# Turning queries with VectorE's 32x32 transposes, and spreading k's maxima through DRAM

## The chip, the cores and the metric

The kernel runs on one core of one Trainium2 chip. The metric is the device time of one execution in microseconds. Three runs of the kernel before gave a median of 943.58 us (943.5 to 944.65).

The engines have these names in the profile: PE is TensorE (matrix products and transposes; PEld its weight loads), DVE is VectorE, ACT is ScalarE, POOL is GpSimd, and SP is the engine whose queue issues nearly all DMAs. SBUF is the on-chip memory with 128 partitions; PSUM holds what PE writes.

## The reference

There are 8 batches, 8 heads, 576 positions and a head width of 64. Queries go through a softmax over the width, keys through a softmax over the positions; there is no attention matrix, only a 64x64 product for each head. The result, 4608 tokens of 512 features, goes through two dense layers with 2048 features between them.

```python
q_s = np.exp(q - np.max(q, axis=-1, keepdims=True))
q_s = q_s / (np.sum(q_s, axis=-1, keepdims=True) + 1e-09)
k_s = np.exp(k - np.max(k, axis=2, keepdims=True))
k_s = k_s / (np.sum(k_s, axis=2, keepdims=True) + 1e-09)
kv = np.einsum('bhsd,bhse->bhde', k_s, v)
x = np.einsum('bhsd,bhde->bhse', q_s, kv)      # then (batch, position) x (head, width)
h = x @ w_in
out = (h * np.clip(h + 3.0, 0.0, 6.0) / 6.0) @ w_out
```

## The kernel before

**Blocks and units.** The 4608 tokens are cut into 9 blocks of 512 (`TB`). As a batch has 576 tokens, block j takes its first 64 j tokens from batch j-1 and the others from batch j. The heads are taken in four pairs, `hp`, of 128 features. One unit, `attention(j, hp)`, does the attention part of one block for one pair of heads. It is a generator, and its `yield`s cut it into steps:

1. It loads k, v and q of the unit, takes k's maxima (`km`) and does the softmax of the queries (`q_softmax`).
2. It subtracts k's maxima from k and takes the exponential, and it turns the queries from tokens x features to features x tokens and splits them into a high and a low part (`qT_hi`, `qT_lo`).
3. It computes `kv` (`kv_of`, ten matmuls into `pkv`, for which the matrix `ke` must be ready).
4. It multiplies `kv` with the turned queries (`px`) and splits the result into `x_hi` and `x_lo`, the input of the dense layers.

**Precision.** Products in the dense layers and, from block 2 on, in step 4 are made of three passes over high and low parts, which `split` makes: ACT writes the high part, DVE (or POOL for some of the weights) subtracts.

**The dense layers.** For each block, 16 groups `f` of 128 hidden features: `gemm1(j, f)` has 12 matmuls into `ph`, then ACT and DVE form the activation `g` (L351, L352) and its parts `g_hi` and `g_lo` (L111, L112). `gemm2`, one group behind, adds 12 matmuls into the four banks `po`. At the end of a block `store` copies the four banks into `ob` (two buffers, by ACT and DVE in turn) and SP sends them out.

**The order of the work.** The units of block j+1 run between the groups of block j, one step for each group: step 1 comes with f = 0, 4, 8 and 12, step 2 with the next f, and so on. Blocks 0 and 1 are "early": block 0's attention comes before everything, block 1's during block 0, while the weights are still being loaded and decoded (`decode`, which uses DVE, ACT and POOL). From block 1 of the dense layers on, PE's instructions stay in the order of the program (`keep_in_program_order`). On all other engines, and on SP's queue, a planner that simulates the times of the instructions sets the order, and it moves work ahead as far as the buffers allow: `kt` and `kb` have one buffer, `ke`, `vt`, `qt` and `km` two. Each engine and SP's queue then run strictly in the order that the planner chose.

**k's maxima, from block 2 on.** k is loaded twice: `kt` with features on the partitions, for the maxima (L286), and `ke` with positions on the partitions, for the product. The maxima come out as one number on each partition, and they are needed along the free dimension on all partitions. POOL copies them to a 128x128 square `kb` (L288), PE transposes it into PSUM as `pm` (L297, through `flip`, L85), and DVE subtracts from `ke` (L298). ACT takes the exponential (L301).

**The queries, from block 2 on.** A tile `qt` has 128 tokens on the partitions and 4 x 128 values in each. `q_softmax` works on groups of 64 values: a maximum (L238), a subtraction (L239), an exponential (L240), a sum (L241), a reciprocal with a small term added (L242, L243) and a multiplication (L244). In step 2 PE transposes the four 128x128 squares into `tp`, and `split` reads them from PSUM.

Of the kernel before, what the change touches and what calls it, by code (L numbers as in the profile page):

```python
# [10 lines left out]
F32 = mybir.dt.float32  # L11
F32R = mybir.dt.float32r
U32 = mybir.dt.uint32
AF = mybir.ActivationFunctionType
ALU = mybir.AluOpType
AX = mybir.AxisListType
PSUM = bass.MemoryType.PSUM

P = 128
TB = 512  # L20
NC4 = TB // P
EPS = 1e-9
LOWEST = float(np.finfo(np.float32).min)
# [6 lines left out]
def attention_moe(  # L30
    ctx: ExitStack,
    tc: tile.TileContext,
    q: bass.AP,
    kT: bass.AP,
    k: bass.AP,
    v: bass.AP,
# [12 lines left out]

    nc = tc.nc

    NB, NP = q.shape[:2]
    B, S = kT.shape[0], kT.shape[3]
    D = q.shape[5]
    NT, DM = out.shape
    NFC = w.shape[0]
    NCC = DM // P
    NTT = TB // P  # L60
    NCH = S // P + 1
    TAIL = S % P
    SHIFT = S - TB

    const = ctx.enter_context(tc.tile_pool(name="const", bufs=1))
    wp = ctx.enter_context(tc.tile_pool(name="wp", bufs=1))
    att = ctx.enter_context(tc.tile_pool(name="att", bufs=1))
    xp = ctx.enter_context(tc.tile_pool(name="xp", bufs=2))
    moe = ctx.enter_context(tc.tile_pool(name="moe", bufs=2))
    ps_a = ctx.enter_context(tc.tile_pool(name="ps_a", bufs=2, space=PSUM))  # L70
    ps_h = ctx.enter_context(tc.tile_pool(name="ps_h", bufs=2, space=PSUM))
    ps_o = ctx.enter_context(tc.tile_pool(name="ps_o", bufs=4, space=PSUM))
# [11 lines left out]
    def flip(out, in_):  # L84
        ordered(nc.tensor.transpose(out, in_, ident))  # L85
# [15 lines left out]

    late = iter(range(NFC - 1, -1, -1))

# [5 lines left out]
    def split(hi, lo, src, engine=nc.vector):  # L109

        nc.scalar.copy(hi, src)  # L111
        engine.tensor_sub(lo, src, hi.bitcast(F32))  # L112
# [44 lines left out]
    def x_block(j):  # L157
        if j not in x_tiles:
            x_tiles[j] = (
                xp.tile([P, NCC, TB], F32R, name=f"x_hi{j}", tag="x_hi"),  # L160
                xp.tile([P, NCC, TB], F32R, name=f"x_lo{j}", tag="x_lo"),
            )
# [13 lines left out]
    def load_first(hp):  # L176
        t = borrow(f"kq{hp}")
        kt, qt, qT = t[:, 0:S], cut(t, S, NC4, 2, D), t[:, S + TB : S + 2 * TB]
        nc.sync.dma_start(kt, kT[0, hp])
# [8 lines left out]
    def kv_of(j, hp, ke, vt):  # L188
# [3 lines left out]
        for c in range(NCH):  # L192
            r = slice(0, P if c < NC4 else TAIL)
            mm(pv, ke[r, c, :], vt[r, c, :, :], c == 0, c == NCH - 1)
# [21 lines left out]

    n8 = 2 * NC4

# [3 lines left out]
    def q_softmax(qt, lean, pool):  # L222

        qs = qt.rearrange("p c h d -> p (c h) d")
        qm = att.tile([P, n8], F32, name="qm", bufs=2)
        qr = att.tile([P, n8], F32, name="qr", bufs=2)
        if lean:
            nc.vector.tensor_reduce(qm, qs, axis=AX.X, op=ALU.max, negate=True)
            for i in range(n8):
                nc.scalar.activation(  # L230
                    qs[:, i],
                    qs[:, i],
                    AF.Exp,
                    bias=qm[:, i : i + 1],
                    accum_out=qr[:, i : i + 1],
                )
        else:
            nc.vector.tensor_reduce(qm, qs, axis=AX.X, op=ALU.max)  # L238
            pool.tensor_sub(qs, qs, over(qm))  # L239
            nc.scalar.activation(qs, qs, AF.Exp)  # L240
            nc.vector.tensor_reduce(qr, qs, axis=AX.X, op=ALU.add)  # L241
        nc.vector.tensor_scalar_add(qr, qr, EPS)  # L242
        nc.vector.reciprocal(qr, qr)  # L243
        pool.tensor_mul(qs, qs, over(qr))  # L244

    def k_softmax(j, km, ke, kt):
# [6 lines left out]
        pe2 = pool.tile([P, TB], F32, name="pe2", tag=tag)  # L253
        for c in range(NC4):
            flip(pe[:, c * P : (c + 1) * P], kt[:, c * P : (c + 1) * P])
        flip(pe2[0:TAIL, 0:P], kt[:, TB:S])
        nc.scalar.copy(ke[:, 0:NC4].rearrange("p c n -> p (c n)"), pe)
        nc.scalar.copy(ke[0:TAIL, NC4], pe2[0:TAIL, 0:P])

    def attention(j, hp):  # L260

        early = j < 2
        if not j:
            kt, qt, qT, vt, ke = first[hp]
        else:
            if j < B:
                kt = att.tile([P, S], F32, name="kt", bufs=1)  # L270
                nc.sync.dma_start(kt, kT[j, hp])
                ke = att.tile([P, NCH, P], F32, name="ke", bufs=2)
                if not early:
                    nc.sync.dma_start(ke, k[j, hp].rearrange("p c h d -> p c (h d)"))
                vt = att.tile([P, NCH, 2, D + 1], F32, name="vt", bufs=2)
                nc.sync.dma_start(vt, v[j, hp])
            qt = att.tile([P, NC4, 2, D], F32, name="qt", bufs=2)
            nc.sync.dma_start(qt, q[j, hp])

        if j < B:  # L280
            km = att.tile([P, 1], F32, name="km", bufs=2)
            if early:
                ks = k_softmax(j, km, ke, kt)
                next(ks)
            else:
                nc.vector.tensor_reduce(km, kt, axis=AX.X, op=ALU.max)  # L286
                kb = att.tile([P, P], F32, name="kb", bufs=1)
                nc.gpsimd.tensor_copy(kb, km.broadcast_to([P, P]))  # L288
        q_softmax(qt, j == 1, nc.vector if j else nc.gpsimd)
        yield  # L290

        if early:
            next(ks, None)
        elif j < B:

            pm = ps_a.tile([P, TB], F32, name="pm", tag="pa")
            flip(pm[:, 0:P], kb)  # L297
            nc.vector.tensor_sub(  # L298
                ke, ke, pm[:, 0:P].rearrange("p (o n) -> p o n", o=1).broadcast_to([P, NCH, P])
            )  # L300
            nc.scalar.activation(ke, ke, AF.Exp)  # L301
        pool, tag = (ps_a, "pa") if j else (ps_o, "po")
        tp = pool.tile([P, TB], F32, name="tp", tag=tag)
        for c in range(NC4):
            flip(tp[:, c * P : (c + 1) * P], qt[:, c].rearrange("p h d -> p (h d)"))
        if early:
            if j:
                qT = att.tile([P, TB], F32, name="qT", tag="qT_hi")
            nc.scalar.copy(qT, tp)
        else:  # L310
            qT_hi = att.tile([P, TB], F32R, name="qT_hi")
            qT_lo = att.tile([P, TB], F32R, name="qT_lo")
            split(qT_hi, qT_lo, tp)
        yield

        if j < B:
            kv_of(j, hp, ke, vt)
            if not early:
                kv_split(j, hp)
            yield  # L320


        pool, tag = (ps_a, "pa") if j else (ps_h, "ph")
        px = pool.tile([P, TB], F32, name="px", tag=tag)
        e = SHIFT * j
        for b, lo, hi in ((j - 1, 0, e), (j, e, TB)):
            if lo < hi:
                c = slice(lo, hi)
                if early:
                    mm(px[:, c], kvs[b, hp], qT[:, c], True, True)  # L330
                else:
                    kv_hi, kv_lo = kvs[b, hp]
                    mm(px[:, c], kv_hi, qT_hi[:, c], True, False)
                    mm(px[:, c], kv_hi, qT_lo[:, c], False, False)
                    mm(px[:, c], kv_lo, qT_hi[:, c], False, True)
        x_hi, x_lo = x_block(j)
        split(x_hi[:, hp, :], x_lo[:, hp, :], px)
        if j == 1:
            kv_split(j, hp)
# [18 lines left out]
    def gemm2(f, g_hi, g_lo, po):  # L358
        first, last = f == 0, f == NFC - 1
        passes = [  # L360
# [50 lines left out]
    for j in range(NB):  # L411
        for f in range(NFC):
            if j == 0:
# [4 lines left out]
            g = gemm1(j, f)  # L418
# [24 lines left out]
def _laid_out(q, k, v, moe_w_in, moe_w_out):  # L443

    B, H, S, D = q.shape
    NP, NCH = H // 2, S // P + 1
    tokens = q.transpose(0, 2, 1, 3).reshape(B * S // TB, NC4, P, NP, 2, D)
    pad = ((0, 0), (0, 0), (0, NCH * P - S), (0, 0))

    def by_chunk(a):  # L450
        return a.reshape(B, NP, 2, NCH, P, a.shape[-1]).transpose(0, 1, 4, 3, 2, 5)

    ones = np.ones((B, H, S, 1), v.dtype)
    n, m = moe_w_in.shape
    w_in = moe_w_in.reshape(n // P, P, m // P, P).transpose(2, 1, 0, 3).reshape(m // P, P, n)
    w = np.stack([w_in, moe_w_out.reshape(m // P, P, n)], axis=2)
    if w.dtype != np.float64:
        raise TypeError(w.dtype)
    return {
        "q": tokens.transpose(0, 3, 2, 1, 4, 5),  # L460
        "kT": k.transpose(0, 1, 3, 2).reshape(B, NP, 2 * D, S),
        "k": by_chunk(np.pad(k, pad, constant_values=LOWEST)),
        "v": by_chunk(np.pad(np.concatenate([v, ones], axis=-1), pad)),
        "w": np.ascontiguousarray(w).view(np.uint64),
    }
# [27 lines left out]
```

## Time and profile before

| what | value |
|---|---|
| median of the runs | 943.58 us |
| the profiled execution's own time | 944.06 us |
| its span, first to last instruction | 942.2 us |
| granted clock, mean | 0.996 |
| PE busy | 915.0 us, 97% |
| DVE busy | 475.9 us, 51% |
| ACT busy | 347.3 us, 37% |
| POOL busy | 34.2 us, 4% |
| chain that ended last | PE 85%, DVE 5% |

The durations in the profile come from the one profiled execution. "Busy" is the share of the span in which an engine had at least one instruction running; matmuls overlap, so the sum of their durations is larger than their share of the time. In a row of the timeline, the brackets hold how long the engine was idle before the instruction and what released it.

### The profile page before, as it was taken

The numbers are of one execution on the slowest core, as the hardware profiler recorded it, in microseconds if no ns is written. First come the engines' busy times: TensorE is split into PE (matmuls) and PEld (weight loads), VectorE is DVE, ScalarE is ACT, GpSimd is POOL, SyncE is SP. The second block draws the span as 40 slices with busy tenths as digits, with TensorE's granted clock in tenths as the row PEclk, the third lists the DMA queues.
The fourth block names the chain that finished last, engine by engine and source line by source line (L and its number), as shares of the span: only waits on it lengthen the run. The fifth ranks groups of instructions, "written<-read, shape, count | busy, mean of one in ns | idle before, by whom it ended". The sixth has DMA issues, their size and how long they took to land.

```text
span 942.2 us, 10586 instructions
## 1 busy us (share of the span) xinstructions
PE 915.0 (97%) x4164; PEld 740.1 (79%) x4164; DVE 475.9 (51%) x823; ACT 347.3 (37%) x599; POOL 34.2 (4%) x49
## 2 busy tenths in 40 slices
PE   5799989999999999999999999999999999999998
PEld 4577767888888888888888888888888888888886
DVE  6999995444444445444544444444444444222222
ACT  6998543223323333333333332323332332222222
POOL 3022110000000000000000000000000000000000
PEclk9999999999999999999999999999999999999999
DMA  9941312111211112111211121112110010001001
GB/s 365 415 187 44 102 35 69 52 52 42 86 51 52 52 52 98 52 52 52 97 53 43 34 97 52 41 41 83 53 40 12 12 56 12 1 1 45 0 1 45
DMA packets 25537, 64.29 MB, mean 68 GB/s; under 512 B 2832, under 2 KB 2832, under 8 KB 23568
## 3 DMA queue, kind: packets, MB, share of 16 engines
q1 hardware_dynamic: 24912, 62.57, 19.1%
q10 hardware_dynamic: 576, 1.05, 0.3%
q8 instruction: 33, 0.54, 0.2%
q14 instruction: 16, 0.13, 0.0%
HBM read 54.17 MB, written 9.44 MB: 68 GB/s over the span
## 4 chain that ended last, share of the span: by engine, by line
PE 85%; DVE 5%; ACT 0%; issue 0%; DVEq 0%; ACTq 0%
PE po L82 39%; PE ph L82 39%; PE pkv L82 3%; PE px L82 2%; PE tp L85 1%; DVE v L141 1%; DVE v L145 1%; DVE m L136 1%; DVE qt L244 0%; DVE m L134 0%; DVE g_lo L112 0%; DVE g L352 0%; PE pm L85 0%; DVE w L112 0%; DVE x_lo L112 0%
## 5 line engine op out<-in xcount | busy, mean ns | idle before, releaser
L82 PE MATMUL ph<-x_hi,w 128*128 128x512 f32 x1152 | 389.1, 399 | 5.4 <-ACT w L111 2.3
L82 PE MATMUL po<-w,g_hi 128*128 128x512 f32 x1152 | 302.1, 400 | 3.8 <-ACT g_hi L111 3.8
L82 PEld LDWEIGHTS ph<-x_hi,w 128*128 128x128 f32 x1152 | 216.9, 189 | 60.4 <-ACT w L111 4.2
L352 DVE SCALAR_TENSOR_TENSOR g<-g,ph 128x512 f32<-128x512 f32 x144 | 98.6, 685 | 322.1 <-ACT g L351 322.1
L82 PEld LDWEIGHTS po<-w,g_hi 128*128 128x128 f32 x1152 | 210.6, 188 | 52.4 <-ACT g_hi L111 5.7
L351 ACT ACTIVATE g<-ph,three 128x512 f32<-128x512 f32 x144 | 98.9, 687 | 395.6 <-PE ph L82 395.6
L82 PE MATMUL ph<-x_lo,w 128*128 128x512 f32 x576 | 228.2, 396 | 0.0
L82 PE MATMUL po<-w,g_lo 128*128 128x512 f32 x576 | 161.6, 394 | 0.0
L82 PEld LDWEIGHTS ph<-x_lo,w 128*128 128x128 f32 x576 | 109.2, 190 | 26.0 <-issue 0.6
L82 PEld LDWEIGHTS po<-w,g_lo 128*128 128x128 f32 x576 | 107.9, 188 | 26.2 <-DVE g_lo L112 0.5
L112 DVE TENSOR_TENSOR g_lo<-g,g_hi 128x512 fp32r<-128x512 f32 x144 | 101.1, 702 | 32.2 <-ACT g_hi L111 29.7
L111 ACT CAST g_hi<-g 128x512 fp32r<-128x512 f32 x144 | 89.3, 620 | 61.0 <-DVE g L352 59.5
L298 DVE TENSOR_TENSOR ke<-ke,pm 128x640 f32<-128x640 f32 x24 | 19.7, 821 | 54.4 <-PE pm L85 54.4
L82 PEld LDWEIGHTS pkv<-vt,ke 128*128 128x128 f32 x280 | 37.4, 189 | 5.8
L82 PE MATMUL pkv<-vt,ke 128*128 128x130 f32 x280 | 41.2, 284 | 0.0
L240 ACT ACTIVATE qt<-qt 128x512 f32<-128x512 f32 x28 | 17.7, 633 | 63.7 <-DVE qt L239 63.7
L241 DVE TENSOR_REDUCE qr<-qt 128x8 f32<-128x512 f32 x28 | 19.2, 685 | 18.2 <-ACT qt L240 18.2
L288 POOL COPY kb<-km 128x128 f32<-128x128 f32 x24 | 7.0, 293 | 564.4 <-PE pm L85 560.8
L112 DVE TENSOR_TENSOR x_lo<-px,x_hi 128x512 fp32r<-128x512 f32 x36 | 24.6, 686 | 0.1
L244 DVE TENSOR_TENSOR qt<-qt,qr 128x512 f32<-128x512 f32 x32 | 24.3, 760 | 0.5
L133 ACT ACTIVATE m<-raw 128x1024 f32<-128x1024 f32 x16 | 18.4, 1147 | 12.3 <-DVE v L141 12.1
L112 POOL TENSOR_TENSOR w<-v,w 128x1024 fp32r<-128x1024 f32 x7 | 17.8, 2541 | 105.3 <-ACT w L111 105.3
(74 smaller groups left out, 547.4 us busy)
## 6 DMA issues: line engine op xcount, KB each, us to landing
raw<-in_w_dram SPq DMA_DIRECT2D x15, 1024.0 KB, 14.7
out_dram<-ob SPq DMA_DIRECT2D x36, 256.0 KB, 2.0
vt<-in_v_dram SPq DMA_DIRECT2D x28, 325.0 KB, 3.5
qt<-in_q_dram SPq DMA_DIRECT2D x32, 256.0 KB, 2.6
kt<-in_kT_dram SPq DMA_DIRECT2D x28, 288.0 KB, 2.8
ke<-in_k_dram SPq DMA_DIRECT2D x24, 320.0 KB, 2.9
kv<-in_v_dram SPq DMA_DIRECT2D x4, 325.0 KB, 6.5
kq<-in_kT_dram SPq DMA_DIRECT2D x4, 288.0 KB, 5.2
```

The costliest lines, as they stand in the source:

```text
L82: ordered(nc.tensor.matmul(out, lhsT, rhs, start=start, stop=stop))
L85: ordered(nc.tensor.transpose(out, in_, ident))
L111: nc.scalar.copy(hi, src)
L112: engine.tensor_sub(lo, src, hi.bitcast(F32))
L133: nc.scalar.activation(m, high.bitcast(F32), AF.Abs)
L136: nc.vector.tensor_scalar(m, m, 3, 0x3FFFFFFF, op0=ALU.logical_shift_left, op1=ALU.bitwise_and)
L240: nc.scalar.activation(qs, qs, AF.Exp)
L241: nc.vector.tensor_reduce(qr, qs, axis=AX.X, op=ALU.add)
L244: pool.tensor_mul(qs, qs, over(qr))
L298: nc.vector.tensor_sub(ke, ke, pm[:, 0:P].rearrange("p (o n) -> p o n", o=1).broadcast_to([P, NCH, P]))
L351: nc.scalar.activation(g, ph, AF.Relu, bias=three, scale=1.0)
L352: nc.vector.scalar_tensor_tensor(g, g, 6.0, ph, op0=ALU.min, op1=ALU.mult)
```

## The change

The change has two parts, both for the units of block 2 and later. Blocks 0 and 1 keep the old way.

**Queries.** They come in another layout, `qf`, prepared outside of the chip as `q` was. Partition 32 r + t holds, for each of 16 groups `g` of 32 tokens, the 32 values of quarter r of the pair's 128 features for token t of that group. Half a head stands on one partition and its other half on the partition 32 away. So the maxima and the sums are taken over 32 values (16 of each per partition), and `both_halves` joins the halves: POOL copies four pieces of 32 partitions to the neighbouring quarter, and DVE combines the result with its own. It is called twice for each unit, for the maxima and for the sums. When the softmax is done, DVE's `transpose` turns each 32x32 square, and the tile has features on the partitions and tokens along the free dimension. Its target `qT` uses buffers of the tag "v", which `decode` uses too. `split` then reads `qT` in SBUF instead of `tp` in PSUM. PE's four transposes and `tp` go.

**k's maxima.** SP writes `km` to a small tile in DRAM (`kd`) and reads it back into `kb` on all 128 partitions. DVE subtracts from `ke` with `kb` as its operand. POOL's copy, PE's transpose and `pm` go.

```diff
+    dr = ctx.enter_context(tc.tile_pool(name="dr", bufs=2, space=bass.MemoryType.DRAM))
...
+    NG = TB // QD
+
+    def across(t):
+        return t.rearrange("p (g o) -> p g o", o=1).broadcast_to([P, NG, QD])
+
+    def both_halves(stat, op):
+        swap = att.tile([P, NG], F32, name="swap", bufs=2)
+        for r in range(0, P, QD):
+            o = r ^ QD
+            nc.gpsimd.tensor_copy(swap[r : r + QD], stat[o : o + QD])
+        nc.vector.tensor_tensor(stat, stat, swap, op=op)
+
+    def q_softmax_t(qt):
+        qs = qt.rearrange("p (g d) -> p g d", d=QD)
+        qm = att.tile([P, NG], F32, name="qm", bufs=2)
+        qr = att.tile([P, NG], F32, name="qr", bufs=2)
+        nc.vector.tensor_reduce(qm, qs, axis=AX.X, op=ALU.max)
+        both_halves(qm, ALU.max)
+        nc.vector.tensor_sub(qs, qs, across(qm))
+        nc.scalar.activation(qt, qt, AF.Exp)
+        nc.vector.tensor_reduce(qr, qs, axis=AX.X, op=ALU.add)
+        both_halves(qr, ALU.add)
+        nc.vector.tensor_scalar_add(qr, qr, EPS)
+        nc.vector.reciprocal(qr, qr)
+        nc.vector.tensor_mul(qs, qs, across(qr))
+        qT = moe.tile([P, 2 * DM], F32, name="v", bufs=2)[:, 0:TB]
+        nc.vector.transpose(qT, qt)
+        return qT
...
-            qt = att.tile([P, NC4, 2, D], F32, name="qt", bufs=2)
-            nc.sync.dma_start(qt, q[j, hp])
+            qt = att.tile([P, TB], F32, name="qt", bufs=2)
+            nc.sync.dma_start(qt, q[j, hp] if early else qf[j - 2, hp])
...
                 nc.vector.tensor_reduce(km, kt, axis=AX.X, op=ALU.max)
+
+                kd = dr.tile([P], F32, name="kd")
+                nc.sync.dma_start(kd.rearrange("(p o) -> p o", o=1), km)
                 kb = att.tile([P, P], F32, name="kb", bufs=1)
-                nc.gpsimd.tensor_copy(kb, km.broadcast_to([P, P]))
-        q_softmax(qt, j == 1, nc.vector if j else nc.gpsimd)
+                nc.sync.dma_start(
+                    kb, kd.rearrange("(o n) -> o n", o=1).broadcast_to([P, P])
+                )
+        if early:
+            q_softmax(qt, j == 1, nc.vector if j else nc.gpsimd)
+        else:
+            qT = q_softmax_t(qt)
         yield
...
-            pm = ps_a.tile([P, TB], F32, name="pm", tag="pa")
-            flip(pm[:, 0:P], kb)
             nc.vector.tensor_sub(
-                ke, ke, pm[:, 0:P].rearrange("p (o n) -> p o n", o=1).broadcast_to([P, NCH, P])
+                ke, ke, kb.rearrange("p (o n) -> p o n", o=1).broadcast_to([P, NCH, P])
             )
...
-            split(qT_hi, qT_lo, tp)
+            split(qT_hi, qT_lo, qT)
```

More of the change, by code (lines that the diff above doesn't have):

```diff
@@ L20 @@
 TB = 512
+QD = 32
 NC4 = TB // P
@@ L33, in attention_moe @@
     q: bass.AP,
+    qf: bass.AP,
     kT: bass.AP,
@@ L52, in attention_moe @@
     nc = tc.nc
-    NB, NP = q.shape[:2]
-    B, S = kT.shape[0], kT.shape[3]
+    B, NP, _, S = kT.shape
     D = q.shape[5]
     NT, DM = out.shape
+    NB = NT // TB
     NFC = w.shape[0]
@@ L276, in attention @@
                 nc.sync.dma_start(vt, v[j, hp])
-            qt = att.tile([P, NC4, 2, D], F32, name="qt", bufs=2)
-            nc.sync.dma_start(qt, q[j, hp])
+            qt = att.tile([P, TB], F32, name="qt", bufs=2)
+            nc.sync.dma_start(qt, q[j, hp] if early else qf[j - 2, hp])
+            if early:
+                qt = qt.rearrange("p (c h d) -> p c h d", c=NC4, h=2)
         if j < B:
@@ L286, in attention @@
                 nc.vector.tensor_reduce(km, kt, axis=AX.X, op=ALU.max)
+                kd = dr.tile([P], F32, name="kd")
+                nc.sync.dma_start(kd.rearrange("(p o) -> p o", o=1), km)
                 kb = att.tile([P, P], F32, name="kb", bufs=1)
-                nc.gpsimd.tensor_copy(kb, km.broadcast_to([P, P]))
-        q_softmax(qt, j == 1, nc.vector if j else nc.gpsimd)
+                nc.sync.dma_start(
+                    kb, kd.rearrange("(o n) -> o n", o=1).broadcast_to([P, P])
+                )
+        if early:
+            q_softmax(qt, j == 1, nc.vector if j else nc.gpsimd)
+        else:
+            qT = q_softmax_t(qt)
         yield
@@ L294, in attention @@
         elif j < B:
-            pm = ps_a.tile([P, TB], F32, name="pm", tag="pa")
-            flip(pm[:, 0:P], kb)
             nc.vector.tensor_sub(
-                ke, ke, pm[:, 0:P].rearrange("p (o n) -> p o n", o=1).broadcast_to([P, NCH, P])
+                ke, ke, kb.rearrange("p (o n) -> p o n", o=1).broadcast_to([P, NCH, P])
             )
             nc.scalar.activation(ke, ke, AF.Exp)
[L302 to L305, printed above, removed]
         if early:
+            pool, tag = (ps_a, "pa") if j else (ps_o, "po")
+            tp = pool.tile([P, TB], F32, name="tp", tag=tag)
+            for c in range(NC4):
+                flip(tp[:, c * P : (c + 1) * P], qt[:, c].rearrange("p h d -> p (h d)"))
             if j:
@@ L459, in _laid_out @@
     return {
-        "q": tokens.transpose(0, 3, 2, 1, 4, 5),
+        "q": tokens[:2].transpose(0, 3, 2, 1, 4, 5),
+        "qf": q.transpose(0, 2, 1, 3)
+        .reshape(B * S // TB, TB // QD, QD, NP, 4, QD)[2:]
+        .transpose(0, 3, 4, 2, 1, 5)
+        .reshape(B * S // TB - 2, NP, P, TB),
         "kT": k.transpose(0, 1, 3, 2).reshape(B, NP, 2 * D, S),
```

## The prediction

> **What bounds the kernel now.** I first read the share of each engine and the granted clock on the page of the kernel before.
>
> ```profile
> PE 915.0 (97%) x4164; PEld 740.1 (79%) x4164; DVE 475.9 (51%) x823; ACT 347.3 (37%) x599; POOL 34.2 (4%) x49
> PEclk9999999999999999999999999999999999999999
> ```
>
> TensorE (PE) works for 97% of the span at an undisturbed clock. An average does not say where the other 3% are, so next comes the table of stretches: span, then busy time of PE, weight loads, VectorE (DVE), ScalarE (ACT), GpSimd (POOL).
>
> ```profile
> 85.00:143.00 58.00, 52.53 (x227) 39.64 (x227) 55.37 (x78) 31.72 (x56) 9.99 (x5) 0.97 0.18 58
> ...
> 156.00:734.00 578.00, 578.00 (x2688) 473.19 (x2688) 272.31 (x515) 183.77 (x309) 6.75 (x23) 1.00 0.18 56
> 734.00:832.00 98.00, 98.00 (x440) 79.58 (x439) 38.91 (x66) 29.64 (x49) 0.00 (x0) 1.00 0.06 19
> ```
>
> From 156 to 832 us PE is busy in every microsecond and waits for nobody, while DVE is at 272.31 of 578.00 and POOL does next to nothing. Before 143 us it is the other way round: DVE is busy for 55.37 of 58.00. So there are two regimes. In the long middle a PE instruction that goes is worth its full time, and new DVE, POOL and DMA work is free so long as it is not late. In the front every DVE instruction counts, and PE instructions hardly do.
>
> **What goes.** The two transposes that the change drops stand in the chain of work that ended last (start, length, what), here in a middle stretch:
>
> ```profile
> 307.60 0.11 PE pm L85
> 307.70 0.44 PE tp L85 x4
> 308.14 2.79 PE po L82 x12
> ...
> 332.71 0.11 PE pm L85
> 332.82 0.44 PE tp L85 x4
> ```
>
> The groups of instructions give their counts and durations, and those of the neighbours that I use for prices below:
>
> ```profile
> L85 PE MATMUL tp<-ident,qt 128*128 128x128 f32 x112 | 16.8, 272 | 0.0
> L111 ACT CAST qT_hi<-tp 128x512 fp32r<-128x512 f32 x28 | 16.2, 577 | 0.0
> L85 PE MATMUL pm<-ident,kb 128*128 128x128 f32 x24 | 6.5, 271 | 0.0
> ...
> L238 DVE TENSOR_REDUCE qm<-qt 128x8 f32<-128x512 f32 x26 | 17.7, 682 | 0.9 <-DMA qt<-in_q_dram 0.8
> L288 POOL COPY kb<-km 128x128 f32<-128x128 f32 x23 | 6.7, 293 | 560.8 <-PE pm L85 560.8
> L243 DVE RECIPROCAL qr<-qr 128x8 f32<-128x8 f32 x26 | 5.1, 197 | 0.2
> ```
>
> The 24 pm transposes (L297's flip of kb) and the 28 x 4 = 112 tp transposes (blocks 2 to 8, four head pairs each) all lie after 150 us, in the regime where PE sets the end. One costs the chain 0.11 us, though its duration reads 272 ns: the instructions overlap, and the time is the step from start to start. So 24 x 0.11 + 28 x 0.44 = 2.64 + 12.32 = **14.96 us** leave. The twelve matmuls behind them keep their 2.79 us, so nothing is handed to the next group. The Trainium skill, "TensorE: Matmul & The Clock Gate", Part 4: PE-mode transpose, gives about 275 ns for a transpose inside a kernel. This trace agrees as a duration (272 ns) and not as a cost.
>
> POOL's 24 copies to kb (0.293 us) go too; POOL was idle, so that is worth nothing.
>
> **What comes in, in the middle.** Per unit (one block, one head pair) DVE gets two small operations on 128x16 (at most 0.197 us each, by the 128x8 reciprocal) and one 32x32-block transpose of 128x512. No row shows that transpose. The nearest are single passes over 128x512 such as L238, 0.682 us; the longest DVE operation of the trace is 2.91 us. I take 0.69; ends 0.6 and 2.91. The Trainium skill, "VectorE: DVE Perf Modes", The three transpose paths, has 311 ns for 128x128 in bf16; four of these would be an estimate of 1.24 us. The rest keeps its size: maxima and sums now run over 32 elements, still 512 per partition; the split and the subtraction of k's maxima read SBUF in place of PSUM. So DVE gains 28 x (0.69 + 0.39) = 30 us over some 676 us of which it idles 365 (578.00 - 272.31 + 98.00 - 38.91). POOL gains 8 copies of 32x16 a unit, at most 0.29 each: 2.3 us. Lateness, not load, is the question. Here is one unit by the clock (start, length, engine):
>
> ```profile
> 433.13 0.82 DVE L298 TENSOR_TENSOR ke<-ke,pm 128x640 f32<-128x640 f32 x1 [2.83 <-PE pm L85]
> 434.46 0.75 DVE L286 TENSOR_REDUCE km<-kt 128x1 f32<-128x576 f32 x1
> 435.72 0.68 DVE L112 TENSOR_TENSOR g_lo<-g,g_hi 128x512 fp32r<-128x512 f32 x1
> 438.93 1.47 PE L82 MATMUL pkv<-vt,ke 128*128 128x130 f32 x10
> 442.30 1.09 PE L82 MATMUL po<-w,g_lo 128*128 128x512 f32 x4
> ...
> 458.17 0.82 DVE L298 TENSOR_TENSOR ke<-ke,pm 128x640 f32<-128x640 f32 x1 [0.72 <-PE pm L85]
> ```
>
> k's maxima of the next unit are there at 434.46 + 0.75 = 435.21, and are first used at 458.17: **23 us** of room. The trip through DRAM is two DMAs in series on SP's queue, the second issued only when the first has landed. The trace has no such trip; its loads and stores, of other sizes, took these medians:
>
> ```profile
> out_dram<-ob SPq DMA_DIRECT2D x36, 256.0 KB, 2.0
> ...
> ke<-in_k_dram SPq DMA_DIRECT2D x24, 320.0 KB, 2.9
> ```
>
> So 4.0 to 5.8 us, and I take 5: well inside 23. If L298 did stand on DVE for kb, the activation chain behind it would stand too. The swap of the maxima and sums makes DVE wait for four POOL copies in a row, twice a unit: 4 x 0.1 to 4 x 0.29 = 0.4 to 1.2 us. Behind it on DVE stands the activation chain (L352, L112), and PE waits for that: g_lo was ready at 435.72 + 0.68 = 436.40 and is used at 442.30, 5.9 us later. 1.2 us vanish in that. The price in the middle is nothing, covered by those 5.9 and 23 us; without them, each microsecond of wait would cost one 24 or 28 times.
>
> A rule of the Trainium skill speaks against this: "SBUF — State Buffer", Who interferes with whom, says that a DVE instruction with two SBUF inputs and a GpSimd instruction that reads SBUF shut each other out for a whole instruction. The trace agrees, in the front below.
>
> **What comes in, in the front.** Part of the work for block 2 already runs there. Chain and GpSimd timeline:
>
> ```profile
> 91.63 2.83 DVE qt L244
> ...
> 109.25 0.11 DVE qr L243
> ...
> 113.88 0.66 DVE km L286
> 114.54 0.59 DVE qm L238
> ```
>
> ```profile
> 91.51 2.40 POOL L112 TENSOR_TENSOR w<-v,w 128x1024 fp32r<-128x1024 f32 x1 [11.81 <-ACT w L111]
> ```
>
> The query softmaxes of two block-2 units (26 of the 28 L238 start after 150 us) and some k maxima are in this DVE-bound stretch, and a DVE multiplication took 2.83 us there, with a 2.40 us POOL split beside it. New there: four small DVE operations (0.11 each as a step, like L243; 0.4); perhaps two subtractions on ke, which no longer wait for PE's pm at its place in PE's order (0.82 each by L298; some 1.5); and a swap copy that gets behind a POOL split, 0 to 2.4 a time. The transposes stay out, since their tile shares "v" with the decoding of the weights and so comes after the last of these. Ends: -2 (the planner moves some of the early softmaxes out of the front; all of those steps together are some 7 us) and +6 (0.4 + 1.5 and two swaps caught for 2.4 each, rounded down). I take **+2**, since DVE is full there.
>
> **Sum.** The profiled execution has a span of 942.2 us and took 944.06, so 1.86 lie around it; the median of the runs is 943.58, 0.48 lower. 942.2 - 14.96 + 2 + 1.86 = 931.1 for such an execution, 930.6 as a median.
>
> **The rivals.**
>
> *Output stores behind the trip.* SP's queue is in order, and two ob buffers wait for it:
>
> ```profile
> 456.76 0.69 DVE L383 TENSOR_SCALAR ob<-po 128x512 f32<-128x512 f32 x1 [1.41 <-DMA out_dram<-ob]
> 458.33 2.10 PE L82 MATMUL po<-w,g_hi 128*128 128x512 f32 x8
> ```
>
> The last ob is written by 457.45, and its bank is wanted by the seventh po matmul, 458.33 + 6 x 0.23 = 459.7: 2.2 us of room, 1.6 without the transposes. If the issue of kb waits on SP for kd to land (2.9 us) plus two issues of 0.33 just ahead of the stores, PE loses 3.6 - 1.6 = 2.0 at each of six block ends that have k work near (blocks 0 to 5): +12 at most, about +6: 937. For it: the order of SP is fixed by the planner's own times. Against: SP is mostly empty.
>
> *Slower: the trip behind a load that stands.* SP waits longest here (waiter, releaser, total, times, longest):
>
> ```profile
> SPq L278 <- PE tp L85: 355.3, 28, 24.8
> ```
>
> That is the load of queries, held until a buffer comes free. If kd and kb are queued behind such a load, the maxima come up to 24.8 + 5.8 = 30.6 us late; the room is 23 us, and 4 more until pkv (L298 ended at 433.95, ke's exponential follows it, pkv begins at 438.93). PE would wait up to 3.6 us in each of 24 units; at half of that, 1.8 x 24 = 43 us, 974. It decides from a loss of 15 / 24 = 0.63 us a unit, that is from about 27.6 us of lateness. Against: qt's buffer is now released by DVE's transpose, not by a place in PE's order, so this wait should shrink.
>
> *Transposes worth their durations.* By 136 x 0.272 = 37 us, less the 2 in front: 908.6. The start-to-start steps of the chain speak against it; only a hidden turnaround of PE could bring it. This is what the transpose page's figure would give if it were a cost.
>
> *No change in the end:* an unseen wait of 0.5 us a unit, such as DVE held by the swap for over 5.9 us, eats the 15: 943. The 1.2 us bound speaks against it.
>
> **How the numbers follow.** Forecast 0.74; stores 0.14 (half of it under 938); trip behind a load 0.07; durations 0.02; no change 0.03. Predicted is the forecast, 930.6. Its own ends are 930.6 - 4 = 926.6 and 930.6 + 4 = 934.6; to leave no more than 2 in 10 out, I go to 926 and, for the stores, to 938. A measurement of this kernel tells about 0.2% (1.9 us) from no change. Faster: forecast, stores and durations, less a little of the stores' far end, 0.89; same 0.03; slower 0.08 (the trip, and that little).
>
> **What would show it.** Right: no pm or tp after block 1; the middle still with PE busy in every microsecond, a unit at 24.5 in place of 25.1 us; DVE near 52% of the middle; kb landing some 5 us after km and long before its subtraction. The front right if PE's unbroken stretch starts about 2 us later than before. Wrong: PE waits for ACT or DVE on g between 156 and 820 us, for po at block ends, or for ke at pkv; a DVE transpose over 3 us; swaps that hold DVE for more than 2 us.

## The result, and the profile after

The changed kernel takes **1115.72 us** (median of four runs, 1114.73 to 1116.81) against 943.87 for the kernel before in the same comparison: 1.182 times as long, 95% interval 1.1802 to 1.1839. The forecast was 930.6, its range 926 to 938. The prediction was wrong, and by far: 15 us were to leave, and 172 came.

The page of the changed kernel, the same two rows as before, and the row of the DMA engines:

```profile
PE 947.8 (85%) x4028; PEld 753.6 (68%) x4028; DVE 504.9 (45%) x907; ACT 348.2 (31%) x599; POOL 73.8 (7%) x249
...
PEclk9999866667666689999999999999999999999999
DMA  9911576576557632111211211121121100000001
```

TensorE (PE) has 4028 instructions, 136 fewer, as predicted, and stands still for 1115.0 - 947.8 = 167.2 us, before 942.2 - 915.0 = 27.2. That is 140 us more waiting. It is also busy for 32.8 us longer although some 15 us of work left, so some 48 us come from slower matmuls. They stand where PE waits: PE's 396 instructions from 120 to 395 us keep it busy for 135 us, and as many take 87 us by the rate of 500 to 700 us below. The granted clock falls there, to 0.67 on average from 170 to 300 us and to 0.50 from 175 to 194 us, and the matmuls of this stretch follow each other mostly in 0.23 or in 0.43 us. 140 + 48 - 15 = 173 us; the span grew by 172.8.

The table of stretches (span, then PE, weight loads, DVE, ACT, POOL, granted clock, share of the DMA engines, GB/s) shows where:

```profile
120.00:170.00 50.00, 21.77 (x64) 15.57 (x64) 21.24 (x32) 9.73 (x14) 3.50 (x5) 0.69 0.64 43
170.00:300.00 130.00, 63.26 (x181) 44.64 (x179) 35.55 (x68) 15.07 (x25) 8.07 (x29) 0.67 0.63 46
300.00:500.00 200.00, 152.51 (x605) 120.94 (x606) 73.13 (x145) 42.89 (x73) 8.39 (x44) 0.83 0.39 44
500.00:700.00 200.00, 200.00 (x913) 162.99 (x912) 99.88 (x197) 65.85 (x109) 12.20 (x64) 1.00 0.16 52
```

From 500 us on the kernel runs as forecast, with PE busy in every microsecond. The loss is between 120 and about 395 us. Over that stretch no engine is busy half of the time, and the DMA engines are, at 0.63, while they move only 46 GB/s; after 500 us they move more, 52 GB/s, at a share of 0.16. So the DMA engines are occupied, and not by bytes. The packet records of the trace put this time on the loads: a packet of 2304 bytes, the size that `kt` is made of, takes 575 ns on average in place of 123 in the kernel before, while those of 4 bytes are recorded with 9 ns each.

The chain of work that ended last, in that stretch (start, length, what):

```profile
162.18 0.32 SPq L330
162.50 0.04 issue
162.55 11.38 DMA kt<-in_kT_dram
...
174.01 0.77 DVE km L327
174.78 0.02 issue
174.80 0.32 SPq L330
175.12 0.04 issue
175.16 11.26 DMA kt<-in_kT_dram
...
186.51 0.76 DVE km L327
```

It is a loop of some 12.5 us. SP writes one unit's maxima to DRAM (L330, `kd`), issues the load of the next unit's k (`kt`, L310), and the load takes 11.3 us. DVE then takes the maxima of that k (L327), which starts the next write. The waits of DVE and PE, and the landing times of the DMAs (median, us), say the same for the whole run:

```profile
DVE km L327 <- DMA kt<-in_kT_dram: 174.3, 23, 10.4
...
PE po L90 <- ACT g_hi L119: 58.1, 12, 9.6
...
PE po L90 <- DVE g_lo L120: 48.1, 9, 8.3
```

```profile
kt<-in_kT_dram SPq DMA_DIRECT2D x28, 288.0 KB, 10.7
ke<-in_k_dram SPq DMA_DIRECT2D x24, 320.0 KB, 2.9
...
kb<-kd SPq DMA_DIRECT2D x24, 64.0 KB, 2.8
...
kd<-km SPq DMA_DIRECT2D x24, 0.5 KB, 8.2
```

The write of 512 **bytes** takes 8.2 us to land, the slowest of all DMAs of the middle but one, and that one is the load issued right behind it. DVE stands for it 23 times, 174.3 us in all. Behind DVE's maxima stand the two operations on the activation, and PE waits for those (58.1 and 48.1 us). All 24 writes lie between 115.0 and 394.8 us: the planner ran the maxima of all units ahead, which also says why the loss ends there. Apart from `kt`'s one buffer nothing held them back: `km` comes free with its write, and the two buffers that `kd` is declared with are no bound either, for between 146.4 and 272.2 us the trace has ten writes to `kd` and no read of it.

The small write has one packet of 4 bytes for each partition, since `km` is a column. The theory to test: **these 4-byte packets hold the DMA queue, and the load behind them stands.** Rivals: the running ahead itself; the number of packets, or any write to DRAM; the queries' part.

### The profile page after: what moved, and what is told of

It is laid out like the page before. It is cut to its first block, busy times and chain, and to the rows that moved or that the text cites. A ratio compares the mean times of both kernels' runs of the same rounds, so it can differ in the third digit from the quotient of the medians.

```text
span 1115.0 us, 10741 instructions
## 1 busy us (share of the span) xinstructions
PE 947.8 (85%) x4028; PEld 753.6 (68%) x4028; DVE 504.9 (45%) x907; ACT 348.2 (31%) x599; POOL 73.8 (7%) x249
## 4 chain that ended last, share of the span: by engine, by line
PE 63%; DMA 23%; DVE 3%; issue 1%; SPq 1%; ACT 0%; POOL 0%; DVEq 0%; ACTq 0%
PE po L90 30%; PE ph L90 29%; DMA kt<-in_kT_dram 22%; PE pkv L90 2%; PE px L90 2%; DVE km L327 2%; DMA ke<-in_k_dram 1%; SPq L330 1%; DVE v L149 0%; DVE qt L252 0%; POOL swap L278 0%; DVE g_lo L120 0%; DVE v L153 0%; DVE g L399 0%; DVE m L144 0%
## 5 line engine op out<-in xcount | busy, mean ns | idle before, releaser
L90 PE MATMUL po<-w,g_hi 128*128 128x512 f32 x1152 | 321.7, 420 | 66.4 <-ACT g_hi L119 58.1
L90 PEld LDWEIGHTS po<-w,g_hi 128*128 128x128 f32 x1152 | 225.7, 200 | 126.1 <-ACT g_hi L119 63.9
L90 PE MATMUL po<-w,g_lo 128*128 128x512 f32 x576 | 171.4, 413 | 48.1 <-DVE g_lo L120 48.1
L327 DVE TENSOR_REDUCE km<-kt 128x1 f32<-128x576 f32 x24 | 18.1, 752 | 174.3 <-DMA kt<-in_kT_dram 174.3
L278 POOL COPY swap<-qm 32x16 f32<-32x16 f32 x112 | 25.4, 227 | 565.5 <-DVE qm L286 547.2
L348 ACT ACTIVATE ke<-ke 128x640 f32<-128x640 f32 x24 | 17.7, 739 | 101.9 <-DVE ke L345 101.9
L286 DVE TENSOR_REDUCE qm<-qt 128x16 f32<-128x512 f32 x28 | 19.1, 682 | 57.4 <-DMA qt<-in_qf_dram 57.4
L345 DVE TENSOR_TENSOR ke<-ke,kb 128x640 f32<-128x640 f32 x24 | 19.8, 826 | 51.6 <-DMA ke<-in_k_dram 50.0
L278 POOL COPY swap<-qr 32x16 f32<-32x16 f32 x112 | 21.7, 194 | 139.5 <-DVE qr L290 135.9
L90 PE MATMUL px<-qT_hi,kv_hi 128*128 128x128 f32 (+7 forms) x52 | 15.9, 305 | 13.8 <-ACT kv_hi L119 13.8
## 6 DMA issues: line engine op xcount, KB each, us to landing
kt<-in_kT_dram SPq DMA_DIRECT2D x28, 288.0 KB, 10.7
```

Of the source, the lines that this page charges most:

```text
L90: ordered(nc.tensor.matmul(out, lhsT, rhs, start=start, stop=stop))
L278: nc.gpsimd.tensor_copy(swap[r : r + QD], stat[o : o + QD])
L345: nc.vector.tensor_sub(ke, ke, kb.rearrange("p (o n) -> p o n", o=1).broadcast_to([P, NCH, P]))
```

## The experiments

All kernels were timed beside the kernel before, which took 943.5 to 944.1 us each time.

**1 and 2. One part at a time.** The changed kernel with the old way for k's maxima, and the kernel before with the new way for k's maxima alone.

```diff
-                kd = dr.tile([P], F32, name="kd")
...
+                nc.gpsimd.tensor_copy(kb, km.broadcast_to([P, P]))
...
+            flip(pm[:, 0:P], kb)
```

> The change's part for the queries alone; k's maxima go through GpSimd and TensorE as before. Theory A (the loss comes from k's maxima: the planner runs all 24 maxima ahead, and each then stands on VectorE behind a kt load that a slow DRAM write holds up): no stretch in which PE waits, 28 x 0.44 = 12.3 us less on PE and 0 to 3 us more in the front, so 931 to 935 us. Rival B (the queries' part, GpSimd's swaps and VectorE's waits for them, makes the loss): above 1000 us.

> The change's part for k's maxima alone; the queries are turned by TensorE as before. Theory A: the whole loss is here, kt loads at about 10.7 us, 1100 to 1135 us. Rival B: 940 to 950 us.

Measured: the queries alone 938.75 us (ratio 0.9946, 0.9931 to 0.996), the maxima alone 1120.36 (1.1871, 1.1848 to 1.1895). The whole loss is in the part with the trip, where `kt` lands in 10.4 us and `kd` in 8.0. The queries' part is a gain, but of 5.0 us and not of the 12.3 that its transposes take in the middle. The stretch from 143 to 156 us, of the kernel before and then with the queries alone, shows a part of the difference:

```profile
143.00:156.00 13.00, 13.00 (x57) 10.54 (x57) 4.08 (x6) 3.76 (x6) 0.16 (x1) 1.00 0.12 46
```

```profile
143.00:156.00 13.00, 9.96 (x39) 7.11 (x40) 10.66 (x19) 3.88 (x7) 5.77 (x16) 1.00 0.14 42
```

DVE has 10.66 us of work there in place of 4.08, and PE loses 3: softmaxes of block 2 pile up in the front.

**3. Running ahead without the trip.** The kernel before, with 24 buffers for `km`, so that its planner may run the maxima ahead.

```diff
-            km = att.tile([P, 1], F32, name="km", bufs=2)
+            km = att.tile([P, 1], F32, name="km", bufs=2 if early else 24, tag="km" if early else "kml")
```

> The kernel before with one edit: 24 buffers for km in place of 2, so that nothing holds the maxima back, and with no trip through DRAM. The planner then puts all 24 maxima ahead, as in the changed kernel. Theory A (running ahead and the slow write are both needed): kt loads in about 3 us, VectorE waits about 3 us at each of some 20 maxima, most of it covered; 944 to 965 us. Rival C (running ahead alone makes the loss): above 1050 us.

Measured: 952.79 us (1.0095, 1.0079 to 1.0112). `kt` lands in 2.8 us, and DVE stands for it

```profile
DVE km L286 <- DMA kt<-in_kT_dram: 20.4, 14, 2.8
```

Running ahead costs 9 us by itself, a twentieth of the loss.

**4. The trip without running ahead.** The changed kernel, where POOL reads `kt` once `kb` has landed, so that the next unit's `kt` can't be loaded sooner.

```diff
+                held = att.tile([P, 1], F32, name="held", bufs=2)
+                nc.gpsimd.tensor_tensor(held, kt[:, 0:1], kb[:, 0:1], op=ALU.add)
```

> The changed kernel, and GpSimd reads one column of kt and of kb after the trip, so that kt's one buffer comes free only when kb has landed; the planner then spreads the maxima over the blocks, with the same slow write. Theory A: PE is busy without a break after the front, 929 to 937 us, though the write to kd still takes 6 us or more to land. Rival D (the slow write hurts wherever it stands): above 1000 us.

Measured: 1129.83 us (1.1973, 1.1955 to 1.1991). My expectation fell: without the running ahead it is no faster. The landing times and waits tell why:

```profile
kt<-in_kT_dram SPq DMA_DIRECT2D x28, 288.0 KB, 2.8
...
qt<-in_qf_dram SPq DMA_DIRECT2D x28, 256.0 KB, 8.2
...
kd<-km SPq DMA_DIRECT2D x24, 0.5 KB, 7.9
```

```profile
DVE qm L286 <- DMA qt<-in_qf_dram: 184.1, 25, 8.9
PE po L90 <- ACT g_hi L119: 126.4, 24, 8.6
```

`kt` is quick again, and the load of the queries is slow, for now this one follows the write on SP's queue. DVE stands for it 25 times in the 28 units, and PE 24 times, 5.3 us each. In both orders it is the load issued within 2.5 us behind the write that stands, and DVE with it.

**5. The same trip in four packets.** DVE turns the column of maxima into rows by one 32x32-block transpose (`km_w`, `km_t`), and the write has 4 packets of 128 bytes.

```diff
-                nc.sync.dma_start(kd.rearrange("(p o) -> p o", o=1), km)
+                nc.vector.transpose(km_t, km_w)
+                nc.sync.dma_start(
+                    kd.rearrange("(r n) -> r n", r=4),
+                    km_t.rearrange("(r n) d -> r n d", r=4)[:, 0],
+                )
```

> The changed kernel, with the maxima turned by a 32x32 transpose on VectorE first, so that they go to DRAM as four packets of 128 bytes in place of 128 packets of 4 bytes. The planner still runs the maxima ahead. Theory E (the write in 4-byte packets occupies the DMA queue for some 8 us, the load behind it lands that much later, and VectorE stands for that load in front of the activations): kt lands in about 3 us, and what stays is the 9 us of running ahead and the front, 938 to 955 us. Rival F (any trip through DRAM does this, or the running ahead together with the queries' part): above 1050 us.

Measured: 940.32 us (0.9965, 0.9953 to 0.9978). The 512 bytes, the trip, SP's queue and the running ahead are all still there; 175 us are gone. The trace has no landing time of `kt` for this run. DVE's waits for it, 174.3 us in the changed kernel, are now

```profile
DVE km_w L333 <- DMA kt<-in_kT_dram: 13.1, 13, 2.1
```

**6. As many packets, but wide.** The changed kernel, where POOL spreads each maximum along its partition and 128 packets of 512 bytes are written and read back. The square isn't turned, so other numbers are subtracted from k; the work is the same.

```diff
-                nc.sync.dma_start(kd.rearrange("(p o) -> p o", o=1), km)
+                nc.gpsimd.tensor_copy(ks, km.broadcast_to([P, P]))
+                kd = dr.tile([P, P], F32, name="kd")
+                nc.sync.dma_start(kd, ks)
```

> The changed kernel, but GpSimd spreads each maximum along its partition, the write takes 128 packets of 512 bytes to DRAM, and kb is read back as it was written: the maxima are not turned, so each row of ke has the wrong number subtracted. Theory E with the size of the packets as the cause: kt lands in about 3 us, 938 to 960 us. Rival G (128 packets of any size written to DRAM, or the write followed by a read, are slow): kt lands in about 10 us, above 1080 us.

Measured: 940.88 us (0.997, 0.9954 to 0.9985).

```profile
kt<-in_kT_dram SPq DMA_DIRECT2D x28, 288.0 KB, 2.9
...
kd<-ks SPq DMA_DIRECT2D x24, 64.0 KB, 2.5
```

128 times the bytes in as many packets, and the write lands in 2.5 us in place of 8.2. So neither the number of packets nor the write to DRAM is slow by itself.

**7. Four sizes side by side.** The kernel before, with an unused write of the first 1, 4, 16 or 128 columns of `kt`, by head pair.

```diff
+                n = (1, 4, 16, P)[hp]
+                kd = dr.tile([P, n], F32, name=f"kd{4 * n}")
+                nc.sync.dma_start(kd, kt[:, 0:n])
```

> The kernel before, unchanged in its work, and beside it in each unit of block 2 and later SP writes the first n columns of kt to a DRAM tile that nothing reads: packets of 4, 16, 64 and 512 bytes for head pairs 0 to 3, always 128 of them. This is the disputed cost by itself. Theory E: the 4-byte writes take some 8 us to land, those of 512 bytes about 2.5 us, and in this order the loads behind them have 20 us of room, so the time stays within 940 to 948 us. Rival J (a slow write costs the kernel whatever stands behind it): 6 units with a 4-byte write at 5 us or more each, above 970 us.

Measured: 949.11 us (1.0056, 1.0041 to 1.0071), a little above what I expected. Most of the 5.1 us more is one wait in the front: the first 4-byte write, which reads `kt`, kept its one buffer for 7.5 us, and DVE waited 4.8 us for the next `kt`. The landing times:

```profile
kd<-kt SPq DMA_DIRECT2D x6, 64.0 KB, 1.5
kd<-kt SPq DMA_DIRECT2D x6, 0.5 KB, 8.4
kd<-kt SPq DMA_DIRECT2D x6, 2.0 KB, 1.4
kd<-kt SPq DMA_DIRECT2D x6, 8.0 KB, 1.4
```

128 packets of 16, 64 or 512 bytes take 1.4 to 1.5 us; of 4 bytes, 8.4. **The 4 bytes are the cause** of the slow landing, and 16 are enough to be rid of it.

The same run shows the load behind the write, in units that differ by the head pair and the width of the packets. After 156 us `ke` and `vt` are issued 1 to 3 us behind each write. Behind the five writes of 4 bytes `ke` lands in 8.8 to 10.7 us and `vt` in 9.3 to 11.2; behind the fifteen wider ones `ke` takes 2.7 to 4.0 and `vt` 3.2 to 5.0. The landing times of `ke` in the kernel before and then in this one:

```profile
DMA to landing us min/median/max: 2.7/2.9/3.5
```

```profile
DMA to landing us min/median/max: 2.7/3.0/10.7
```

The delay is about as long as if a load began only when the write has landed. An estimate from the rows: in the changed kernel 8.2 - 0.4 + 2.8 = 10.6 us for a `kt` issued 0.4 us behind the write (10.7 measured), and in experiment 4 7.9 - 2.5 + 2.6 = 8.0 us for a `qt` issued 2.5 us behind (8.2 measured). What on the way holds the load, no run shows.

In the middle these writes cost PE nothing (it is busy for 300.00 of 300 us from 200 us on), since here no load that is needed at once comes behind them.

The Trainium skill, "DMA: Bandwidth & Descriptors", Specifications, gives 512 bytes as the smallest transfer at line rate, because below it the engine reads, modifies and writes. The landing times agree with a price below 512 bytes for 4 bytes alone; at 16 and 64 they show none. That the engine reads, modifies and writes, no trace here can show.

**8 to 11. What the rest costs.** In the changed kernel DVE's last use frees the buffers of `kt` and `qt`. Before, PE's transposes held them to a fixed place in PE's order: `tp` freed `qt`, and `pm` freed `kb`, without which POOL could not free `km` for the next maximum of a `kt`. These kernels give back such a place, by a POOL instruction that reads the buffer late: for `kt` with four packets, as in experiment 4; for the queries alone; for the queries with four packets; and for queries and maxima, both behind `qT_lo`, which ACT and DVE make in step 2.

```diff
+            if j < B:
+                held_k = att.tile([P, 1], F32, name="held_k", bufs=2)
+                nc.gpsimd.tensor_tensor(held_k, km_w[:, 0:1], qT_lo[:, 0:1].bitcast(F32), op=ALU.add)
+            held_q = att.tile([P, 1], F32, name="held_q", bufs=2)
+            nc.gpsimd.tensor_tensor(held_q, qt[:, 0:1], qT_lo[:, 0:1].bitcast(F32), op=ALU.add)
```

> Four packets, and kt held until kb has landed, as in the run with the hold alone (1129.83 us). Theory E: no load lands late and nothing runs ahead, 934 to 941 us: the queries' part alone had 938.75, and 2.6 us of PE for pm go. Rival F: above 1000 us.

> The queries' part alone (938.75 us), and GpSimd reads one column of qt and of qT_lo after the split, so that qt's buffers come free at the same place in PE's order as when TensorE read them. Theory H (of the 12.3 us, some 7 were given back because qt came free early and several softmaxes of block 2 pile up before the first output copies): the first copy to ob moves ahead of them, 932 to 936 us. Rival I (VectorE's and GpSimd's greater work in the front costs them wherever it stands): 938 to 940 us.

> The changed kernel with the write in four packets (940.32 us) and qt held until the split, as in the queries' run (935.86 us); the maxima still run ahead. If the two gains add, 935 to 938 us; if the run of maxima in the front is what costs now, 939 to 944 us.

> As the run before, and GpSimd also reads km beside qT_lo in step 2, so that the maxima are held back at the place in PE's order where pm had held them. Both parts of the change are then there, without the slow write and without running ahead: 935.86 less the 2.6 us of pm, 931 to 936 us. If VectorE's waits for loads that the planner puts just ahead of it cost something (as in the run with kt held, 954.42 us): 938 to 956 us.

Measured: `kt` held until `kb` lands, 954.42 (1.0106, 1.0091 to 1.0121), a miss. Three loads then come right ahead of their use (DVE waits 54.8 us for `kt`, 63.2 for `qt` and 29.0 for `ke`), and PE loses 5.4 of 300 us in the middle: this hold costs more than none (940.32). Queries held, 935.86 (0.9913, 0.9899 to 0.9928), as expected in the time; but from 120 to 156 us PE is busy for 30.09 us, against 29.68 in experiment 1, so that the front is the reason for the gain isn't shown. Queries held with four packets and the maxima running ahead, 944.10 (1.0005, 0.9995 to 1.0014): no gain, and why this hold costs 3.8 us against 940.32 stays open. Both held, **920.90** (0.9757, 0.9743 to 0.9772), 10 us better than I had expected, and most of that was not the hold.

**12 and 13. The place in SBUF.** With both held, twelve matmuls follow each other in 2.72 us, also after 840 us, where no attention work is left; the kernel before takes 2.80 there. The helper tiles push x, g and their parts to other addresses. So: the kernel before with unused tiles that give it those addresses, and the kernel with both held with 128 bytes per partition more.

```diff
+    for i in range(2):
+        nc.gpsimd.memset(const.tile([P, 32], F32, name=f"pad{i}"), 0.0)
+    nc.gpsimd.memset(att.tile([P, 160], F32, name="pad_att"), 0.0)
```

> The kernel before, with three unused tiles in front (256 bytes and 640 bytes per partition), so that the weights, x, g and their low parts lie at the byte addresses that they have in the kernel with both parts held. No other instruction is changed but three memsets. Theory P (the place of the operands in SBUF sets the pace of the matmuls: there 12 matmuls of 512 columns took 2.72 us, in all other traces 2.78 to 2.80): a group takes 2.72 us here too, and the kernel, of which TensorE is some 98% busy, 943.9 x 2.72/2.80 = about 917 to 924 us. Rival Q (the faster pace comes from something else in that kernel): 2.80 us a group and 943 to 945 us.

> The kernel with both parts held, with one unused tile of 128 bytes per partition in front, so that x and g lie at another address (800 instead of 672 beyond a multiple of 1024, as in the kernel before). Theory P: 12 matmuls take 2.78 to 2.80 us again, and the kernel 932 to 938 us, which is what both parts are worth without the place. Rival Q: 2.72 us a group and 920 to 922 us.

Measured: the kernel before, moved, **928.69** us (0.9841, 0.9825 to 0.9858); the kernel with both held, moved, 937.38 (0.9936, 0.9919 to 0.9952). The chain near the end, of the kernel before, of the same moved, and of the one with both held, moved:

```profile
843.43 2.80 PE po L82 x12
846.22 2.80 PE ph L82 x12
```

```profile
841.62 2.72 PE po L82 x12
844.34 2.72 PE ph L82 x12
```

```profile
841.03 2.80 PE po L90 x12
843.83 2.80 PE ph L90 x12
```

The pace goes with the addresses, in both directions and with the same instructions; the first run is 4 to 5 us above its expectation, so the size was not met there. From start to start over some 170 matmuls it is 226.7 ns in the two kernels at the good addresses, and 232.4 to 233.1 ns in the thirteen others. Which address makes the difference isn't settled: a whole set of tiles was moved.

## Why the prediction was wrong

**PE's transposes: right.** All 136 left, and each was worth its step and not its duration. The groups of matmuls between 156 and 880 us, of the kernel before and then of the one with both held, moved, which has the same pace:

```profile
L82 PE MATMUL ph<-x_hi,w 128*128 128x512 f32 x930 | 310.6, 394 | 0.0
L82 PE MATMUL po<-w,g_hi 128*128 128x512 f32 x936 | 245.5, 400 | 0.0
L82 PE MATMUL ph<-x_lo,w 128*128 128x512 f32 x466 | 183.6, 394 | 0.0
L82 PE MATMUL po<-w,g_lo 128*128 128x512 f32 x468 | 130.8, 393 | 0.0
```

```profile
L90 PE MATMUL ph<-x_hi,w 128*128 128x512 f32 x952 | 317.8, 394 | 0.0
L90 PE MATMUL po<-w,g_hi 128*128 128x512 f32 x952 | 248.6, 398 | 2.6 <-ACT g_hi L124 2.2 <-DVE ob L447 0.2 <-ACT ob L449 0.2
L90 PE MATMUL ph<-x_lo,w 128*128 128x512 f32 x476 | 187.5, 394 | 0.0
L90 PE MATMUL po<-w,g_lo 128*128 128x512 f32 x476 | 133.7, 394 | 0.0
```

2800 matmuls before, 2856 after: 56 x 0.233 = 13.0 us gained in the same 724 us, against the 14.96 of the forecast. Of the 1.9 missing, 0.5 are PE waits in this stretch (the other 2.1 of the 2.6 in the row lie before 156 us); the rest I can't place. With the queries alone held the count is 2852, at its pace of 0.2326: 52 x 0.2326 = 12.1 against 12.32. So the rival by durations (908.6) falls.

**DVE's and POOL's new work: right.** The rows of the changed kernel:

```profile
L296 DVE STREAM_TRANSPOSE v<-qt 128x512 f32<-128x512 f32 x28 | 19.7, 704 | 0.0
...
L279 DVE TENSOR_TENSOR qr<-qr,swap 128x16 f32<-128x16 f32 x28 | 4.8, 173 | 19.8 <-POOL swap L278 19.8
L279 DVE TENSOR_TENSOR qm<-qm,swap 128x16 f32<-128x16 f32 x28 | 4.8, 172 | 8.8 <-POOL swap L278 8.8
```

The transpose takes 0.704 us, 0.69 taken. (The estimate of 1.24 from the Trainium skill, "VectorE: DVE Perf Modes", The three transpose paths, was too high.) DVE waits 19.8 / 28 + 8.8 / 28 = 1.0 us a unit for the swaps, inside the 0.4 to 1.2. From 500 us on this costs PE nothing. In the kernel with both held, moved, the same waits come to 27.8 and 20.7 us, 1.7 a unit: above the range, but PE is still busy for 299.84 of 300 us from 200 us on.

**The trip: the step that failed.** "So 4.0 to 5.8 us, and I take 5: well inside 23" and "The price in the middle is nothing". Two things were wrong in it. The size: I priced `kd` by a store of 256 KB and a load of 320 KB, though it has 4 bytes per partition; it landed in 8.2 us in place of 2.0 to 2.9. And the place, which weighs more: 8.2 + 2.8 = 11 us are still well inside 23, and `kb` was in truth hardly ever waited for (1.5 us, twice). I asked only when the trip's own data are late. What came late was **the load queued behind the write**, `kt` at 10.7 us in place of 2.8, which I had not looked at; experiments 5 to 7 show that the 4-byte packets do it. Behind it came a price that the sum did not have at all: where PE waited, the clock fell, and slower matmuls are some 48 us of the loss.

The 23 us of room were also not a property of the new kernel. They held while PE's `pm` freed `kb` once a unit. The change took that gate away, the planner put all 24 maxima into the time up to 395 us, and so each write got a load right behind it that DVE needed next.

**The front.** +2, with ends -2 and +6, was low but held: PE's busy time from 120 to 156 us is 20.24 + 13.00 = 33.24 before, 29.32 with both parts held, moved (+3.9), and 30.09 with the queries held (+3.2).

**The rivals.** "The trip behind a load that stands" (974) had the side of the result and the right queue, but the wrong order: the loads stood behind the trip. Output stores behind the trip: DVE and ACT waited 9.5 and 20.6 us for `ob`, small against the 174.3. No change (943) has the time of the kernel with four packets and the queries held (944.10), but not, as far as is shown, its reason.

**What the idea is worth.** With packets of 128 bytes and with the old gates given back, both parts gain 943.48 - 937.38 = 6.1 us at the old addresses and 928.69 - 920.90 = 7.8 us at the good ones (from two comparisons, in which the kernel before differs by 0.5 us). PE's 13.0 us in the middle less the 3.9 of the front would be 9.1; the spans of the two profiled executions differ by 942.2 - 934.2 = 8.0. The rest is open. The kernel with both held, at 920.90 us, beats both kernels of this case, but two thirds of its gain are the 14.8 us that the addresses give to the kernel before alone.

## What to carry to other kernels

Here the width of the packets set the price of a small write, not its bytes and not the number of packets, and those who paid were the loads issued just behind it: ask who stands behind a DMA, not only whether its own data arrive in time. A column of one number per partition makes 4-byte packets; turn it before it goes to DRAM. By the landing times 16 bytes of each partition would do as well, but no run tried that in the changed kernel. When an instruction with a fixed place goes, look what it was gating, since a planner will run work ahead into the gap.

## What the hardware showed that I had not expected

- 128 packets of 4 bytes to DRAM take 8.4 us to land, and of 16, 64 and 512 bytes 1.4, 1.4 and 1.5. A 288 KB load issued behind the 4-byte write took 10.7 us in place of 2.8, with the DMA engines 63% busy at 46 GB/s. In one kernel, `ke` took 8.8 to 10.7 us behind the 4-byte writes and 2.7 to 4.0 behind the wider ones.
- The same matmuls run at 226.7 or 233.1 ns from start to start, 2.8% apart, by where the tiles lie in SBUF: 14.8 us of this kernel for three unused tiles. Among the thirteen kernels at other addresses the pace differed by up to 0.3%, some 2 us here, so differences of that size between two of these kernels are not put down to their edits.
